# A chunked decay attention with an eight-expert mixture: w1 gathered in two parts, the filling products taken out, the experts' order fitted anew

## The chip, the cores and the metric

One core of a Trainium2 chip runs the program. The metric is the device time of one launch in microseconds (us). Five engines work side by side, each through a queue of its own in a fixed order: TensorE (PE, matrix products; PEld are its weight loads), VectorE (DVE), ScalarE (ACT), GpSimd (POOL) and SyncE (SP, which only issues transfers here). Semaphores hold an instruction until what it needs is done.

## The reference

Two parts. The first is a linear attention with a complex decay, for B=4, H=8, S=768 positions and D=48; its output, as `x`, has N=3072 tokens of 384 numbers. The second sends each token to one of eight experts, each of which takes exactly `cap` = 384 tokens.

```python
for t in range(S):
    S_re, S_im = ar*S_re - ai*S_im + kv, ar*S_im + ai*S_re
    y[:, :, t] = einsum('bhd,bhde->bhe', q[:, :, t], S_re)
x = y.transpose(0, 2, 1, 3).reshape(3072, 384)
for idx in argsort(-(x @ w_gate).flatten()):       # best score first
    tok, e = idx // 8, idx % 8
    if assigned[tok] < 0 and counts[e] < 384:
        assigned[tok] = e; counts[e] += 1
for e in range(8):
    out[assigned == e] = relu(x[assigned == e] @ w1[e]) @ w2[e]
```

`w1[e]` is 384 x 1024 and `w2[e]` 1024 x 384, in 32-bit floats.

## The kernel before, in words

**Attention (0 to some 228 us).** 24 pieces of 128 tokens. The recurrence over positions becomes products of blocks on TensorE. `store` (line 608) writes each piece's `x` to the array `xd` in DRAM, 128 rows of 384 numbers, from GpSimd for the first 21 pieces; the logits stay on the chip.

**Ranking.** The greedy rule is solved one expert after another, in the order in which the experts fill up, so which expert comes first is known only on the chip. `Router.find` (line 830) searches the score from which an expert takes all tokens, in rounds of 32 thresholds. In a round VectorE compares every token's key with the thresholds (`ind`), TensorE counts per expert and threshold (`cnt`), VectorE makes flags and their sum (`f`, `fm`), and TensorE adds the step to the thresholds of the next round (`thr`). For the first expert `ind` is made in three pieces, so that counting starts sooner. After the rounds follow the expert's number (`eidx`, as a row number for each of 128 partitions), ties, and each token's place (`pi`). `Router.slots` (line 1030) turns places into lists of 384 token numbers, `idx`: VectorE builds one-hot factors (`hl`, `o`, `rh`), TensorE multiplies them (`cnt`), VectorE adds four partial sums where the product came in four groups (`ic`, four steps) and casts to integers (`idx`).

**Gathers.** `route` (line 1350) issues an expert's transfers on GpSimd, all indirect: `w1t`, one row of 3 x 1024 numbers for each of 128 partitions (1.57 MB), by `eidx`; three times 128 token rows from `xd`, by a column of `idx` each (`xg`); and `w2t`, 1.57 MB by `eidx`, for experts 0 to 2 after the rows.

**First expert.** `first_expert` (line 1419) works in plain 32-bit floats, 128 tokens at a time: `turn` transposes the rows on TensorE against `ident`, ScalarE copies them (`x`); `hidden` multiplies with `w1t`, eight blocks of 128 hidden features with three products each; `last` multiplies with `w2t`, and GpSimd scatters the rows to `out`. A plain 32-bit product runs as two passes, so its record counts twice (x6 for three products).

**Experts 1 to 7.** 384 tokens at once. Each operand is split in a high and a low part (`split`: ScalarE makes the high one, VectorE subtracts), and a product is three products of these parts: `xh,w1h`, `xl,w1h`, `xh,w1l`, then `w2h,hl` and so on. `w1` is split in three pieces of 1024 columns, one for each third of the 384 input features, so all three pieces must be there before a block of hidden features is complete.

**Filling and warm-up products.** `fill` (line 788) puts products of one constant into a spare accumulator, behind which the next useful product is made to wait. `FILLS` (line 1508) gives the numbers: 24 before the first round; in each round 5 after the counts and 7 after the new thresholds, 14 after the last ones; and 36 while VectorE makes places. `WARM` = 14 (line 1507) products of `mask` with `ident` stand between the first slot products and the first turn, the loop being at line 1466. Nobody reads the result of either.

**What sets the order.** In the expert half every operation is recorded (all at line 140) with its estimated duration. `rank` gives each a due time by the way that remains behind it, less an offset by its kind from the table `M_OFF` (line 1503; kinds are `find3`, `slot2`, `w1s`, `tp` and so on). `in_order` then plays the engines through and issues on each the ready operation with the smallest number. So the table decides which of two ready steps comes first, on every engine. The attention has a table of its own, which the change leaves alone.

Of the kernel before, what the change touches and what calls it, by code (L numbers as in the profile page):

```python
# [8 lines left out]
F32 = mybir.dt.float32  # L9
# [13 lines left out]
N, DM, E, FF = B * S, H * D, 8, 1024  # L23
CAP = N // E
NT = N // 128
GC = 3
T = GC * 128
FK = FF // 128
# [218 lines left out]
def attention(nc, real, tc, z, kq_in, a_re, a_im, v_in, xd, later):  # L247
# [261 lines left out]
    def unit(i):  # L509
# [204 lines left out]
class Router:  # L714
# [72 lines left out]

    def fill(self, n, after):

        with self.nc.one():  # L790
            for _ in range(n):
                self.nc.tensor.matmul(self.hot, self.z.tri, self.z.tri, start=True, stop=True)
        o = self.nc.ops[-1]
        o.kind = "fill"
        if after is not None:
            o.deps.append(after)
        self.filled = [o]

    def scale(self):
# [30 lines left out]
    def find(self, parts, by_pe, more):  # L830
# [5 lines left out]
        def t(n, shape, dt=F32, **k):  # L836
            return wk.tile(shape, dt, name=n, **k)
# [7 lines left out]
        if first:  # L845
            begin()
            self.fill(FILLS[0], nc.ops[-1])
        thr = self.thr
        lots = list(zip(parts, parts[1:] + (NT,)))
        for it in range(len(GRID)):  # L850
# [3 lines left out]
            for n, (lot, stop) in enumerate(lots):  # L854
                some = ind[:, lot:stop]
                some.part = n
                v.tensor_tensor(some, bc(m[:, lot:stop], 32),
                                thr[:, None, 32 * it:32 * it + 32].to_broadcast([128, stop - lot, 32]), op=OP.is_ge)
                with nc.one() as group:
# [22 lines left out]
            for lo, hi in ((at, at + 32), (at + 32, end + 1)) if first and at < end else ((at, end + 1),):  # L882
                nc.tensor.matmul(thr[:, lo:hi], self.weight[:, it].to_broadcast([128, 128]), fm_.bitcast(BF)[:, 1:2].to_broadcast([128, hi - lo]),
                                 start=False, stop=(it == len(GRID) - 1), skip_group_check=True)
                if first:
                    nc.ops[-1].deps += self.filled
            if first:
                self.fill(FILLS[2 if at < end else 3], nc.ops[-1])

# [19 lines left out]
        v.tensor_scalar(s1, self.pidm, lop[:32], lo[:32], op0=OP.add, op1=OP.is_equal)  # L909
        with nc.one() as group:  # L910
            if not by_pe:
                closing()
            counts()
        if first:
            group[0].deps += self.filled
            nc.kind = "lead"
# [29 lines left out]
        nc.tensor.matmul(off, z.tri, rt.rearrange("p a b -> p (a b)").bitcast(BF)[:, 1::2], start=True, stop=True)  # L946
        if first:
# [82 lines left out]
    def slots(self, pi, by_pe):  # L1030
# [19 lines left out]
        for h in range(2):  # L1050
# [9 lines left out]
            self.placed = group[0]  # L1060
            if self.filled:
                group[0].deps += self.filled
        self.filled = []
        idx = t("idx", [128, 3], I32, bufs=8)
# [216 lines left out]
def experts(nc, tc, z, router, w1, w2, xd, out):  # L1281
# [50 lines left out]
    hot = pm.tile([128, 3, 128], F32, name="acc", bufs=5)  # L1332
    router.hot = hot[:, 0]
    idx, w1s, w2t, latest = {}, {}, {}, []

    w1t0 = wp.tile([128, 3, FF], F32, name="w1t", bufs=2)
    xg0 = wk.tile([128, 3, DM], F32, name="xg")
# [12 lines left out]
    def route(e):  # L1350
# [8 lines left out]
        eidx, pi = router.found  # L1359
        w1t = w1t0 if e == 0 else wp.tile([128, 3, FF], F32, name="w1t", bufs=2)  # L1360
# [52 lines left out]
    def settle():  # L1413
# [3 lines left out]
        settled.append(o)  # L1417

    def first_expert(xg):

# [10 lines left out]
        def hidden(j):  # L1431
            for f0 in range(0, FK, 3):
                n = min(3, FK - f0)
                hp = pm.tile([128, 3, 128], F32, name="acc", bufs=5)
                for i in range(n):
                    col = slice((f0 + i) * 128, (f0 + i) * 128 + 128)
                    with plan.one():
                        whole(hp[:, i], [(w1s[0][:, kk, col], x0[:, j][:, kk]) for kk in range(3)])
                act(h0[:, j][:, f0:f0 + n], hp[:, :n], AF.Relu).kind = "h"
# [34 lines left out]
    for e in range(1, E):  # L1474
# [4 lines left out]
        for f in range(FK):  # L1479
            hp = pm.tile([128, CAP], F32, name="acc", bufs=5)  # L1480
            col = slice(f * 128, f * 128 + 128)
            product(hp, [([w[:, kk, col] for w in w1s[e]], [x[:, kk] for x in xs]) for kk in range(3)], True)
            hi, lo = (h[:, f] for h in hs)
# [18 lines left out]
M_LATE = 0.0  # L1502
M_OFF = {'close1': 4907.3801, 'close2': 3736.7957, 'close3': 12989.3501, 'close4': 4978.9595, 'close5': 20150.8396, 'close6': 7935.2835, 'find1': 910.3797, 'find2': -491.2383, 'find3': 12453.3585, 'find4': 936.189, 'find5': 1287.5239, 'find6': -3522.5781, 'find7': 2244.6658, 'fill': -40000.0, 'first': 30000.0, 'lead': 31000.0, 'h': -9561.514, 'mm': -23392.8927, 'next0': 2441.5673, 'next1': 11732.2633, 'next2': -9507.9749, 'next3': 3444.9243, 'next4': -9522.1411, 'next5': -1772.7047, 'next6': 766.1226, 'ot': 6939.8479, 'out': 3884.4579, 'place1': 5375.3134, 'place2': -4569.1293, 'place3': 4573.9198, 'place4': 7290.1175, 'place5': 798.3189, 'place6': 454.7009, 'slot1': 5720.6654, 'slot2': 3387.2087, 'slot3': -8030.2154, 'slot4': 6878.5738, 'slot5': -5200.2856, 'slot6': -10123.2603, 'slot7': -5245.0693, 'tp': -28295.1209, 'w1d': 3587.4164, 'w1s': -39661.3634, 'w2d': 14744.4273, 'w2s': -204656.3808, 'warm': -8694.1139, 'x': -5392.4881, 'xd': 5339.4823}
W1_POOL = ()
M_SLACK = 0.4
W2_POOL = {}
WARM = 14
FILLS = (24, 5, 7, 14, 36)
PARTS = ((0, 8, 16),) + 6 * ((0,),)
# [5 lines left out]
@with_exitstack  # L1515
def tile_decay_attention_then_capacity_moe(ctx, tc, kq, a_re, a_im, v, w_gate, w1, w2, out):
    nc = tc.nc
# [8 lines left out]
    attention(queue, nc, tc, z, kq, a_re, a_im, v, xd, router.constants())  # L1526
    experts(queue, tc, z, router, w1, w2, xd, out)


def _lay_out(inputs):  # L1530
# [7 lines left out]
    def in_pieces(a):  # L1538
# [4 lines left out]
    c = np.ascontiguousarray  # L1543
    v = inputs["v"].transpose(0, 1, 3, 2).reshape(B, 4, 2 * D, S // T, T).transpose(0, 3, 2, 1, 4)
    return {
        "kq": c(np.stack([feature_major(inputs["k"]), feature_major(inputs["q"])], axis=2)).reshape(G, 128, 6 * T),
# [3 lines left out]
        "w_gate": c(inputs["moe_w_gate"]).reshape(4, 2, D, E),  # L1550
        "w1": c(inputs["moe_w1"].reshape(E, 3, 128, FF).transpose(0, 2, 1, 3)).reshape(E * 128, 3 * FF),
        "w2": c(inputs["moe_w2"].reshape(E, FK, 128, DM).transpose(0, 2, 1, 3)).reshape(E * 128, FK * DM),
# [16 lines left out]
```

## Time and profile before

| | |
|---|---|
| three runs | 504.97, 505.26, 506.15 us (median 505.26) |
| profiled execution, its own time | 505.34 us |
| its span, from first to last instruction | 503.6 us |
| TensorE busy | 464.3 us (92%), 5284 instructions |
| TensorE weight loads | 406.2 us (81%) |
| VectorE busy | 406.6 us (81%) |
| ScalarE busy | 285.1 us (57%) |
| GpSimd busy | 84.3 us (17%) |

The shares are averages over stages with different limits, and products that nobody reads count as busy. "Granted clock" is the share of TensorE's full speed that the chip allows in a stretch: 1.00 stands for 2.4 GHz, 0.50 for 1.2 GHz. A row of a timeline reads: start, duration, engine, line, operation, result and operands with their shape, how many instructions are taken together, and in brackets how long the engine was idle before and what released it.

### The profile page before, as it was taken

To read this page: it belongs to the slowest core of one execution; us is meant where nothing else is said; L and a number is where in the kernel's file an instruction comes from. 1 tells how busy PE (TensorE), PEld (TensorE's weight loads), DVE (VectorE), ACT (ScalarE), POOL (GpSimd) and SP (SyncE) were. 2 spreads that over 40 slices of the span, in tenths; PEclk is the share of its full clock that TensorE was granted. 3 is DMA by queue.
4 is the path that set the end of the run, shared out by engine and by line. 5 is a ranking of instruction groups with operands and counts; after the bars stand their busy time and mean duration, and the time that the engine had idled before them with its cause. 6 is when DMAs were issued, how large, how long until landed. Compare 5 with 4: busy or idle time off the path is not lost.

```text
span 503.6 us, 12840 instructions
## 1 busy us (share of the span) xinstructions
PE 464.3 (92%) x5284; PEld 406.2 (81%) x5284; DVE 406.6 (81%) x1172; ACT 285.1 (57%) x470; POOL 84.3 (17%) x120
## 2 busy tenths in 40 slices
PE   0488999999999999998889999999999999999995
PEld 0276888888787988887888689888988889989995
DVE  7989999999999999636846799799898998937250
ACT  7999988999998974710021443154423444345341
POOL 2000000000010000000210411424121252350202
PEclk9999999999999999998799999999999999999999
DMA  7647877868578664520340723562070621780001
GB/s 269 202 143 192 302 243 215 267 208 291 170 214 283 223 189 126 162 81 19 140 159 1 268 79 134 191 240 94 33 297 33 267 79 45 278 316 21 31 17 48
DMA packets 26538, 82.70 MB, mean 164 GB/s; under 512 B 4096, under 2 KB 11136, under 8 KB 23408
## 3 DMA queue, kind: packets, MB, share of 16 engines
q1 hardware_dynamic: 19264, 42.55, 27.6%
q0 software_dynamic: 6784, 38.75, 21.4%
q8 instruction: 41, 0.67, 0.6%
q10 hardware_dynamic: 432, 0.59, 0.3%
q14 instruction: 17, 0.14, 0.1%
HBM read 53.49 MB, written 9.44 MB: 125 GB/s over the span
## 4 chain that ended last, share of the span: by engine, by line
PE 49%; DVE 18%; issue 13%; ACT 10%; DMA 4%; POOL 2%; SPq 1%; POOLq 1%; another core or an unknown queue 0%; DVEq 0%; ACTq 0%
PE acc L140 21%; PE y L140 7%; PE U L140 6%; PE sc L140 6%; ACT s L140 3%; PE vx L140 3%; PE sq L140 3%; DVE hl L140 2%; DVE f L140 2%; PE kp L140 2%; PE cnt L140 2%; ACT L271 2%; DMA w2t<-in_w,eidx 2%; DMA ai<-in_a_im 2%; POOL out L140 2%
## 5 line engine op out<-in xcount | busy, mean ns | idle before, releaser
L140 ACT ACTIVATE hh<-acc 128x384 fp32r<-128x384 f32 x56 | 27.5, 491 | 72.3 <-PE acc L140 71.8
L140 PE MATMUL acc<-w2h,hl 128*128 128x384 f32 x168 | 54.4, 346 | 0.0
L140 PE MATMUL acc<-w2l,hh 128*128 128x384 f32 x168 | 53.8, 346 | 0.5 <-DVE w2l L140 0.3
L140 PE MATMUL acc<-w2h,hh 128*128 128x384 f32 x168 | 53.9, 345 | 0.0
L140 PE MATMUL acc<-xh,w1h 128*128 128x384 f32 x168 | 52.3, 347 | 1.0 <-ACT w1h L140 0.7
L140 PE MATMUL acc<-xh,w1l 128*128 128x384 f32 x168 | 51.8, 346 | 0.0
L140 PE MATMUL sc<-KQ 96*128 96x128 f32 x384 | 50.4, 281 | 1.2 <-DVE am L140 1.2
L140 PE MATMUL acc<-xl,w1h 128*128 128x384 f32 x168 | 51.3, 343 | 0.0
L140 PEld LDWEIGHTS sc<-KQ 96*128 96x128 f32 x384 | 45.7, 191 | 5.0 <-DVE am L140 1.6
L140 POOL DMA_DIRECT2D xd<-x x21 | 11.4, 545 | 193.0 <-ACT LP L140 161.8
L140 PE MATMUL y<-vt,am 128*64 128x56 f32 x768 | 43.6, 224 | 0.0
L140 DVE SCALAR_TENSOR_TENSOR hl<-acc,hh 128x384 fp32r<-128x384 f32 x56 | 30.7, 551 | 15.7 <-ACT hh L140 14.3
L140 POOL DMA_INDIRECT out<-ot,idx x24 | 26.9, 1122 | 97.8 <-ACT ot L140 95.6
L140 DVE TENSOR_TENSOR f<-kq,CS 128x768 f32<-128x768 f32 x48 | 42.5, 949 | 0.5 <-ACT CS L140 0.3
L140 DVE TENSOR_TENSOR ind<-m,thr 128x768 bf16<-128x768 f32 (+1 forms) x45 | 34.0, 773 | 10.1 <-PE thr L140 7.7
L140 PEld LDWEIGHTS y<-vt,am 128*64 128x64 f32 x768 | 36.8, 137 | 3.9 <-issue 2.3
L140 PE MATMUL y<-W,KQ 96*64 96x56 f32 x640 | 38.5, 222 | 0.5 <-DVE W L140 0.5
L140 PE MATMUL sq<-s,ident 128*128 128x384 f32 x42 | 20.1, 563 | 17.3 <-ACT sq L140 17.3
L140 DVE TENSOR_TENSOR am<-sc,mask 128x512 f32<-128x512 f32 x48 | 31.9, 682 | 4.6 <-PE sc L140 4.2
L140 POOL DMA_INDIRECT xg<-xd,idx x24 | 25.9, 1078 | 51.6 <-DVE idx L140 24.8
L140 PEld LDWEIGHTS acc<-xh,w1h 128*128 128x128 f32 x168 | 31.1, 188 | 2.7 <-ACT w1h L140 1.0
L140 PEld LDWEIGHTS y<-W,KQ 96*64 96x64 f32 x640 | 32.6, 137 | 0.6 <-DVE W L140 0.6
(201 smaller groups left out, 1135.2 us busy)
## 6 DMA issues: line engine op xcount, KB each, us to landing
KQ<-f SPq DMA_DIRECT2D x64, 192.8 KB, 4.1
kq<-in_kq SPq DMA_DIRECT2D x8, 1152.0 KB, 8.6
KQ<-f SPq DMA_DIRECT2D x64, 96.4 KB, 3.1
V<-in_v SPq DMA_DIRECT2D x8, 576.0 KB, 4.9
xd<-x POOLq DMA_DIRECT2D x21, 192.0 KB
ar<-in_a_re SPq DMA_DIRECT2D x6, 576.0 KB, 4.4
ai<-in_a_im SPq DMA_DIRECT2D x6, 576.0 KB, 5.4
ar<-in_a_re SPq DMA_DIRECT2D x2, 384.0 KB, 3.2
```

The costliest lines, as they stand in the source:

```text
L140: r = f(*a, **k)
L271: real.scalar.add_instruction(ins)
```

## The change

- **w1 in two arrays.** The host lays `w1` out by pairs of hidden blocks: four chunks of 768 numbers for each partition, each with all three thirds of the input features for two hidden blocks. The first three chunks are the array `w1a`, the last is `w1b`. `route` gathers each by an indirect transfer of its own (1.18 and 0.39 MB). `weight(w, f, kk)` picks a block's factor.
- **The first expert's second part** is issued behind the first 128 token rows, and the other rows behind it; the order w1a, rows, w1b, rows, rows, w2 is forced by dependences. The later experts issue w1b right behind w1a.
- **Splits of w1** in four pieces of 768 columns, in place of three of 1024.
- **No filling products**: `fill`, `FILLS` and the waits behind them are gone.
- **Warm-up products** 10 in place of 14.
- **Two VectorE steps** (`e2`, `rs`) are written ahead of `of` in the ranking.
- **The first two stores** of `x` go in halves of 64 rows.
- **M_OFF** has other numbers throughout, and no `fill`.

```diff
         def store():
-            (nc.gpsimd if i < NT - 3 else nc.scalar).dma_start(xd[i * 128:i * 128 + 128], mine["x"].rearrange("p a b -> p (a b)"))
+            for a in (0, 64) if i < 2 else (0,):
+                b = a + 64 if i < 2 else 128
+                (nc.gpsimd if i < NT - 3 else nc.scalar).dma_start(
+                    xd[i * 128 + a:i * 128 + b], mine["x"][a:b].rearrange("p a b -> p (a b)"))
...
         if first:
             begin()
-            self.fill(FILLS[0], nc.ops[-1])
...
-                if first:
-                    group[0].deps += self.filled
-            if first:
-                self.fill(FILLS[1], nc.ops[-1])
...
-            if first:
-                self.fill(FILLS[2 if at < end else 3], nc.ops[-1])
...
         nc.tensor.matmul(off, z.tri, rt.rearrange("p a b -> p (a b)").bitcast(BF)[:, 1::2], start=True, stop=True)
-        if first:
-            self.fill(FILLS[4], nc.ops[-1])
-        of = t("of", [128, 2])
-        v.tensor_copy(of, off)
...
         v.scalar_tensor_tensor(rs, cc, -1.0, e2, op0=OP.mult, op1=OP.mult, accum_out=r)
+        of = t("of", [128, 2])
+        v.tensor_copy(of, off)
...
-        rows(w1t.rearrange("p a f -> p (a f)"), w1, eidx, 128 * 3 * FF * 4, "w1d")
+        def part(lo, hi):
+            def issue():
+                nc.gpsimd.indirect_dma_start(out=flat.real()[:, 768 * lo:768 * hi], out_offset=None, in_=w1[lo // 3],
+                                             in_offset=bass.IndirectOffsetOnAxis(ap=eidx.real(), axis=0))
+            move(issue, [w1t[:, c] for c in range(lo, hi)], [eidx], 128 * 768 * (hi - lo) * 4, "w1d")
+            return plan.ops[-2]
+        part(0, 3)
         if late:
             plan.ops[-2].deps.append(late)
+        if e:
+            part(3, 4)
...
             rows(xg[:, j], xd, i[:, j:j + 1], 128 * DM * 4, "xd")
+            if e == 0 and j == 0:
+                before = plan.ops[-2]
+                before = [before, part(3, 4)]
+                before[1].deps.append(before[0])
+            elif e == 0:
+                plan.ops[-2].deps.append(before[1])
...
-            w1s[e] = pair([128, 3, FF], "w1", 2)
-            for kk in range(3):
-                split(w1t[:, kk], *(w[:, kk] for w in w1s[e]), "w1s", g if (e, kk) in W1_POOL else v)
+            w1s[e] = pair([128, 4, 768], "w1", 2)
+            for c in range(4):
+                split(w1t[:, c], *(w[:, c] for w in w1s[e]), "w1s", g if (e, c) in W1_POOL else v)
...
+    def weight(w, f, kk):
+        at = (f % 2 * 3 + kk) * 128
+        return w[:, f // 2, at:at + 128]
...
-M_OFF = {..., 'fill': -40000.0, 'first': 30000.0, 'lead': 31000.0, 'h': -9561.514, 'mm': -23392.8927, ...}
+M_OFF = {..., 'first': -763.0821, 'h': -11761.0629, 'lead': 6417.3714, 'mm': -11170.5708, ...}
...
-WARM = 14
-FILLS = (24, 5, 7, 14, 36)
+WARM = 10
```

Three places show how the order moves. The first is TensorE's queue from the last counts of the second expert's first round to the first expert's first products. `mask` against `ident` are warm-up products, `ident,xg` the three transposes of the first 128 rows, `thr` the second expert's new thresholds. Ahead of these rows both kernels have eight more warm-up records. Before:

```order
L140 MATMUL cnt<-oh,ind 128x32
L140 MATMUL acc<-ident,mask 128x128 x6
L140 MATMUL acc<-ident,xg 128x128
L140 LDWEIGHTS weight
L140 MATMUL thr<-fm_163,weight 128x129
L140 MATMUL acc<-ident,xg 128x128 x2
L140 MATMUL acc<-x_3791,w1t 128x128 x3
```

With the change:

```order
L140 MATMUL cnt<-oh,ind 128x32
L140 MATMUL acc<-ident,mask 128x128 x2
L140 MATMUL acc<-ident,xg 128x128 x3
L140 LDWEIGHTS weight
L140 MATMUL thr<-fm_163,weight 128x129
L140 MATMUL acc<-x_3657,w1t 128x128 x6
L140 LDWEIGHTS ind
```

Four warm-up products fewer stand before the transposes, and the three transposes now stand together ahead of `thr`.

The second is GpSimd's queue at the first expert's gathers. Before, with the second expert's `w1t` behind them:

```order
L140 DMA w1t<-in_w,eidx 128x3072
L140 DMA xg<-xd,idx 128x384 x3
L140 DMA w2t<-in_w,eidx 128x3072
L140 DMA w1t<-in_w,eidx 128x3072
L140 DMA out<-ot,idx 3072x384
```

With the change:

```order
L140 DMA w1t<-in_w1a,eidx 128x2304
L140 DMA xg<-xd,idx 128x384
L140 DMA w1t<-in_w1b,eidx 128x768
L140 DMA xg<-xd,idx 128x384 x2
L140 DMA w2t<-in_w,eidx 128x3072
L140 DMA w1t<-in_w1a,eidx 128x2304
L140 DMA w1t<-in_w1b,eidx 128x768
L140 DMA out<-ot,idx 3072x384
```

Two issues more stand ahead of the first scatter, one of them between the first rows and the others.

The third is VectorE's queue where the third expert's (expert 2's) slot sums `ic` become `idx`. `hl` is the low part of expert 1's hidden features, `w2l` that of its second weights, `cs` and `f` belong to the ranking of the expert after. Before:

```order
L140 TENSOR_TENSOR ic<-cnt,ic 32x12
L140 SCALAR_TENSOR_TENSOR hl<-acc,hh 128x384
L140 TENSOR_TENSOR cs_167<-cnt,need 32x8
L140 SCALAR_TENSOR_TENSOR hl<-acc,hh 128x384
L140 TENSOR_TENSOR cs_167<-cnt,cs_167 32x8
L140 SCALAR_TENSOR_TENSOR hl<-acc,hh 128x384
L140 TENSOR_TENSOR cs_167<-cnt,cs_167 32x8
L140 TENSOR_TENSOR w2l<-w2t,w2h 128x384
L140 TENSOR_TENSOR cs_167<-cnt,cs_167 32x8
L140 TENSOR_TENSOR w2l<-w2t,w2h 128x384
L140 TENSOR_SCALAR f_159,fm_163<-cs_167 32x8
L140 CAST idx<-ic 32x3 x4
```

With the change:

```order
L140 TENSOR_SCALAR ic<-cnt 32x12
L140 TENSOR_TENSOR oh<-oh,free 128x192
L140 TENSOR_TENSOR ic<-cnt,ic 32x12
L140 SCALAR_TENSOR_TENSOR hl<-acc,hh 128x384
L140 TENSOR_TENSOR ic<-cnt,ic 32x12
L140 SCALAR_TENSOR_TENSOR hl<-acc,hh 128x384
L140 TENSOR_TENSOR ic<-cnt,ic 32x12
L140 SCALAR_TENSOR_TENSOR hl<-acc,hh 128x384
L140 CAST idx<-ic 32x3 x4
```

The cast moved up ahead of the ranking's four `cs` and its `f` and of two `w2l`; one `hl` is left between the last sum and the cast.

## Rows read from the trace of the kernel before

**Rows 1.** Busy time by stretch: us, busy (instructions) per engine, clock, DMA, GB/s.

```profile
230.50:235.70 5.20, 4.99 (x96) 4.20 (x97) 4.15 (x22) 0.00 (x0) 0.22 (x2) 1.00 0.08 27
235.70:246.00 10.30, 10.28 (x148) 9.42 (x146) 7.44 (x51) 0.00 (x0) 1.02 (x1) 0.50 0.05 14
246.00:255.50 9.50, 6.23 (x87) 5.67 (x86) 6.54 (x27) 0.49 (x1) 3.82 (x4) 1.00 0.73 246
255.50:296.00 40.50, 40.12 (x294) 31.64 (x295) 28.57 (x124) 13.43 (x28) 7.51 (x8) 1.00 0.38 135
296.00:498.00 202.00, 197.76 (x1269) 182.29 (x1268) 155.62 (x574) 79.93 (x162) 55.55 (x51) 1.00 0.37 132
```

**Rows 2.** Timeline of VectorE, first ranking: start us, us, instruction, idle before and releaser.

```profile
233.82 1.08 DVE L140 TENSOR_TENSOR ind<-m,thr 128x256 bf16<-128x256 int32 x3 [0.24 <-PE thr L140]
...
235.44 0.07 DVE L140 DVE_READ_ACCUMULATOR f<-cnt 32x1 f32 x1
...
235.82 1.08 DVE L140 TENSOR_TENSOR ind<-m,thr 128x256 bf16<-128x256 int32 x3 [0.23 <-PE thr L140]
...
237.46 0.07 DVE L140 DVE_READ_ACCUMULATOR f<-cnt 32x1 f32 x1
...
238.07 1.08 DVE L140 TENSOR_TENSOR ind<-m,thr 128x256 bf16<-128x256 int32 x3 [0.46 <-PE thr L140]
...
246.64 0.30 DVE L140 TENSOR_TENSOR rh<-o,token 128x288 f16<-128x288 f16 x1
```

**Rows 3.** Timeline of TensorE, first ranking to second turn, same columns.

```profile
235.57 0.21 PE L140 MATMUL thr<-fm,weight 128*128 128x32 bf16 x2
...
237.77 0.26 PE L140 MATMUL thr<-fm,weight 128*128 128x32 bf16 x2
...
247.35 0.76 PE L140 MATMUL cnt<-rh,o 128*32 128x12 f16 x24
...
248.04 2.05 PE L140 MATMUL acc<-ident,mask 128*128 128x128 f32 x16
...
251.67 0.32 PE L140 MATMUL cnt<-oh,ind 128*128 128x32 bf16 x6 [1.57 <-DVE ind L140]
...
253.42 0.39 PE L140 MATMUL acc<-ident,xg 128*128 128x128 f32 x2
...
255.50 0.94 PE L140 MATMUL acc<-x,w1t 128*128 128x128 f32 x6 [1.69 <-ACT x L140]
...
261.68 0.74 PE L140 MATMUL acc<-ident,xg 128*128 128x128 f32 x5
```

**Rows 4.** Timeline of GpSimd, gathers of the first expert.

```profile
243.93 1.02 POOL L140 DMA_INDIRECT w1t<-in_w,eidx  x1 [12.25 <-DVE tie L140]
249.07 0.98 POOL L140 DMA_INDIRECT xg<-xd,idx  x1 [4.12 <-DVE idx L140]
250.35 0.95 POOL L140 DMA_INDIRECT xg<-xd,idx  x1 [0.30 <-issue]
```

**Rows 5.** Busy time by stretch, columns as in rows 1: weight gather.

```profile
248.50:249.50 1.00, 1.00 (x12) 1.00 (x11) 0.92 (x4) 0.00 (x0) 0.43 (x1) 1.00 0.94 393
```

**Rows 6.** Timeline of ScalarE, copies of turned rows.

```profile
254.96 0.49 ACT L140 ACTIVATE x<-acc 128x384 f32<-128x384 f32 x1 [25.54 <-PE acc L140]
...
262.13 0.87 ACT L140 ACTIVATE x<-acc 128x384 f32<-128x384 f32 x2
```

**Rows 7.** Waits of TensorE from 296 to 498: us in total, times, longest.

```profile
PE acc L140 <- DMA xg<-xd,idx: 0.9, 1, 0.9
PE acc L140 <- ACT w1h L140: 0.7, 1, 0.7
```

**Rows 8.** Timeline of TensorE in expert 1, which turns expert 2's rows.

```profile
319.28 0.44 PE L140 MATMUL acc<-ident,xg 128*128 128x128 f32 x2 [0.93 <-DMA xg<-xd,idx]
```

**Rows 9.** Timeline of VectorE before expert 2's row gathers.

```profile
311.01 0.54 DVE L140 TENSOR_TENSOR w2l<-w2t,w2h 128x384 fp32r<-128x384 f32 x1
...
311.55 0.67 DVE L140 CAST idx<-ic 32x3 int32<-32x3 f32 x4
```

More of the change, by code (lines that the diff above doesn't have):

```diff
@@ L786, in mine @@
         return self.nc.wrap(self.con.tile(shape, dt, name=n), dt)
[L788 to L797, printed above, removed]
     def scale(self):
@@ L858, in find @@
                                 thr[:, None, 32 * it:32 * it + 32].to_broadcast([128, stop - lot, 32]), op=OP.is_ge)
-                with nc.one() as group:
+                with nc.one():
                     for c in range(0, stop - lot) if by_pe else ():
@@ L884, in find @@
                                  start=False, stop=(it == len(GRID) - 1), skip_group_check=True)
-                if first:
-                    nc.ops[-1].deps += self.filled
-            if first:
-                self.fill(FILLS[2 if at < end else 3], nc.ops[-1])
         def closing():
@@ L909, in find @@
         v.tensor_scalar(s1, self.pidm, lop[:32], lo[:32], op0=OP.add, op1=OP.is_equal)
-        with nc.one() as group:
+        with nc.one():
             if not by_pe:
@@ L914, in find @@
         if first:
-            group[0].deps += self.filled
             nc.kind = "lead"
@@ L946, in find @@
         nc.tensor.matmul(off, z.tri, rt.rearrange("p a b -> p (a b)").bitcast(BF)[:, 1::2], start=True, stop=True)
-        if first:
-            self.fill(FILLS[4], nc.ops[-1])
-        of = t("of", [128, 2])
-        v.tensor_copy(of, off)
         r = t("r", [128, 1])
@@ L1060, in slots @@
             self.placed = group[0]
-            if self.filled:
-                group[0].deps += self.filled
-        self.filled = []
         idx = t("idx", [128, 3], I32, bufs=8)
@@ L1332, in experts @@
     hot = pm.tile([128, 3, 128], F32, name="acc", bufs=5)
-    router.hot = hot[:, 0]
     idx, w1s, w2t, latest = {}, {}, {}, []
-    w1t0 = wp.tile([128, 3, FF], F32, name="w1t", bufs=2)
+    w1t0 = wp.tile([128, 4, 768], F32, name="w1t", bufs=2)
     xg0 = wk.tile([128, 3, DM], F32, name="xg")
@@ L1359, in route @@
         eidx, pi = router.found
-        w1t = w1t0 if e == 0 else wp.tile([128, 3, FF], F32, name="w1t", bufs=2)
+        w1t = w1t0 if e == 0 else wp.tile([128, 4, 768], F32, name="w1t", bufs=2)
         late = e == E - 1 and latest[-1]
-        rows(w1t.rearrange("p a f -> p (a f)"), w1, eidx, 128 * 3 * FF * 4, "w1d")
+        flat = w1t.rearrange("p a f -> p (a f)")
+        def part(lo, hi):
[5 more added lines that the diff above has]
+        part(0, 3)
         if late:
             plan.ops[-2].deps.append(late)
+        if e:
+            part(3, 4)
         def second():
@@ L1435, in hidden @@
                 for i in range(n):
-                    col = slice((f0 + i) * 128, (f0 + i) * 128 + 128)
                     with plan.one():
-                        whole(hp[:, i], [(w1s[0][:, kk, col], x0[:, j][:, kk]) for kk in range(3)])
+                        whole(hp[:, i], [(weight(w1s[0], f0 + i, kk), x0[:, j][:, kk]) for kk in range(3)])
                 act(h0[:, j][:, f0:f0 + n], hp[:, :n], AF.Relu).kind = "h"
@@ L1480, in experts @@
             hp = pm.tile([128, CAP], F32, name="acc", bufs=5)
-            col = slice(f * 128, f * 128 + 128)
-            product(hp, [([w[:, kk, col] for w in w1s[e]], [x[:, kk] for x in xs]) for kk in range(3)], True)
+            product(hp, [([weight(w, f, kk) for w in w1s[e]], [x[:, kk] for x in xs]) for kk in range(3)], True)
             hi, lo = (h[:, f] for h in hs)
@@ L1502 @@
 M_LATE = 0.0
-M_OFF = {'close1': 4907.3801, 'close2': 3736.7957, 'close3': 12989.3501, 'close4': 4978.9595, 'close5': 20150.8396, 'close6': 7935.2835, 'find1': 910.3797, 'find2': -491.2383, 'find3': 12453.3585, 'find4': 936.189, 'find5': 1287.5239, 'find6': -3522.5781, 'find7': 2244.6658, 'fill': -40000.0, 'first': 30000.0, 'lead': 31000.0, 'h': -9561.514, 'mm': -23392.8927, 'next0': 2441.5673, 'next1': 11732.2633, 'next2': -9507.9749, 'next3': 3444.9243, 'next4': -9522.1411, 'next5': -1772.7047, 'next6': 766.1226, 'ot': 6939.8479, 'out': 3884.4579, 'place1': 5375.3134, 'place2': -4569.1293, 'place3': 4573.9198, 'place4': 7290.1175, 'place5': 798.3189, 'place6': 454.7009, 'slot1': 5720.6654, 'slot2': 3387.2087, 'slot3': -8030.2154, 'slot4': 6878.5738, 'slot5': -5200.2856, 'slot6': -10123.2603, 'slot7': -5245.0693, 'tp': -28295.1209, 'w1d': 3587.4164, 'w1s': -39661.3634, 'w2d': 14744.4273, 'w2s': -204656.3808, 'warm': -8694.1139, 'x': -5392.4881, 'xd': 5339.4823}
+M_OFF = {'close1': 21139.6573, 'close2': 7314.2043, 'close3': 12942.22, 'close4': 11690.8262, 'close5': 6863.2998, 'close6': -451.5483, 'find1': -3704.0335, 'find2': -1916.3891, 'find3': -67.7544, 'find4': 4806.073, 'find5': -1681.1192, 'find6': -3654.3032, 'find7': -11609.9588, 'first': -763.0821, 'h': -11761.0629, 'lead': 6417.3714, 'mm': -11170.5708, 'next0': -5975.6657, 'next1': -4106.9594, 'next2': -158.233, 'next3': -10211.75, 'next4': -5088.7055, 'next5': -17234.0147, 'next6': -1009.421, 'ot': 401.8857, 'out': 333.4749, 'place1': 6801.0462, 'place2': 6417.4987, 'place3': 8870.8733, 'place4': 6634.6636, 'place5': -9432.3868, 'place6': 7743.1919, 'settle': 7563.6529, 'slot1': 12159.7359, 'slot2': 1416.9124, 'slot3': 5587.3936, 'slot4': -2743.7043, 'slot5': 3927.6614, 'slot6': 8368.2895, 'slot7': 7183.0966, 'tp': -37525.3228, 'w1d': 7842.4279, 'w1s': -24592.7515, 'w2d': 1176.6931, 'w2s': -21874.9893, 'warm': -5299.0651, 'x': -2358.03, 'xd': 1891.4784}
 W1_POOL = ()
@@ L1515, in tile_decay_attention_then_capacity_moe @@
 @with_exitstack
-def tile_decay_attention_then_capacity_moe(ctx, tc, kq, a_re, a_im, v, w_gate, w1, w2, out):
+def tile_decay_attention_then_capacity_moe(ctx, tc, kq, a_re, a_im, v, w_gate, w1a, w1b, w2, out):
     nc = tc.nc
@@ L1526, in tile_decay_attention_then_capacity_moe @@
     attention(queue, nc, tc, z, kq, a_re, a_im, v, xd, router.constants())
-    experts(queue, tc, z, router, w1, w2, xd, out)
+    experts(queue, tc, z, router, (w1a, w1b), w2, xd, out)
 def _lay_out(inputs):
@@ L1544, in _lay_out @@
     v = inputs["v"].transpose(0, 1, 3, 2).reshape(B, 4, 2 * D, S // T, T).transpose(0, 3, 2, 1, 4)
+    w1 = inputs["moe_w1"].reshape(E, 3, 128, FK, 128).transpose(0, 2, 3, 1, 4).reshape(E * 128, 3 * FF)
     return {
@@ L1550, in _lay_out @@
         "w_gate": c(inputs["moe_w_gate"]).reshape(4, 2, D, E),
-        "w1": c(inputs["moe_w1"].reshape(E, 3, 128, FF).transpose(0, 2, 1, 3)).reshape(E * 128, 3 * FF),
+        "w1a": c(w1[:, :2304]),
+        "w1b": c(w1[:, 2304:]),
         "w2": c(inputs["moe_w2"].reshape(E, FK, 128, DM).transpose(0, 2, 1, 3)).reshape(E * 128, FK * DM),
```

## The prediction

> **What bounds the kernel now.** I read the busy time by stretch first, to see which stretch has which limit. From 296 us to the end of the products TensorE is busy for 197.76 of 202.00 us [rows 1]: the seven later experts are a queue on TensorE, and only a wait inside that queue can be won there. The first expert (255.5 to 296) is the same, 40.12 of 40.50. Between 230.5 and 255.5, where tokens are ranked and the first expert's rows fetched, the same column tells nothing, because up to 246 most of TensorE's work is filling products, which nobody reads. There I read VectorE's timeline. One round of the ranking is: three `ind` pieces, their counts on TensorE, `f`, and `thr`, which starts the next round. Rounds start at 233.82, 235.82 and 238.07 [rows 2]: 2.00 us, then 2.25. The granted clock explains the step only in part: it is 1.00 (2.4 GHz) up to 235.7, 0.50 (1.2 GHz) from there to 246, and 1.00 again [rows 1]. It fell while the short fills (5 and 7) ran between the counts, and rose after the long ones (14 and 36).
>
> After the ranking three steps follow in a row: the slot products `cnt` give `idx`; GpSimd issues the row gathers from `idx`; TensorE turns the first 128 rows, ScalarE copies them (`x`), and the first expert's products begin at 255.50 [rows 3]. That start is what the first half of the change can move. From there on TensorE is a queue, so what starts earlier should end earlier.
>
> **The change, part by part.** The sum is made against the profiled execution's own 505.34 us; the median of the runs shown is 505.26, so 0.08 lies between them.
>
> *Stores in halves.* The first two stores become four, on GpSimd, which does little else in the first half; nobody waits for them there: 0.
>
> *Fills in the rounds.* In the quick round `fm` is read out from 235.44 to 235.51 and `thr` starts at 235.57, 0.06 later; in the slow one it is ready at 237.53 and `thr` starts at 237.77, 0.24 later, because five fills at the lower clock stand ahead of it [rows 2, 3]. Without fills each of the three rounds at the lower clock gets 0.18 back: 0.54. The clock will fall earlier, since TensorE now does less; the two quick rounds then pay what the slow one pays besides the fills, 2.25 - 2.00 - 0.18 = 0.07 each, 0.14. Net gain 0.40.
>
> *Fills before the slot products.* `rh` is ready at 246.94 but the 24 products start at 247.35, behind 36 fills [rows 2, 3]. Free of them they start at about 247.0 and end some 0.3 earlier (their second half waits for one more VectorE step). One short VectorE step (`open`, about 0.1) now stands ahead of this chain: net 0.2. The row gathers come 0.40 + 0.2 = 0.6 earlier: the issue at 249.07 moves to 248.5 [rows 4].
>
> *The weight gather.* Now it is issued at 243.93, and the stretch from 248.5 to 249.5 moves 393 GB/s [rows 4, 5]. Its index moves up too, ahead of four VectorE steps. A quarter of 1.57 MB less is 0.39 MB, or 1.0 us; with the 0.6 above the first part is in about 1.6 us before the whole is now, and the first rows no longer queue behind it: they land before TensorE asks. The second part (chunk 4 of 4, for the last two of eight hidden blocks) is issued 1.3 us after the first rows and needed some 4 us into the products: hidden. The rows for the second and third turn, and `w2t`, go out 1.3 later against 0.6 earlier; the second turn comes 6 us after the first products [rows 3], so this is hidden too, and costs up to 0.7 if that cover goes.
>
> *Warm-up products.* 28 half-products (16 + 12) become 20 (16 + 4). 16 ran in 2.05 us at the upper clock, with their start [rows 3]. Now the clock is at its lower level when they begin, near 247.6, so 16 take up to 3.6 us and end at 251.2. That is about when the next ranking's `cnt` may start (251.67 less 0.6). Then that group, four half-products and the three transposes, all at the lower clock, 0.3 + 0.9 + 0.6: the transposes end at 253.0, where they end at 253.81 now [rows 3]. Gain 0.8.
>
> *The pause before `x`.* The transposes' rows end at 253.81, yet ScalarE is released only at 254.96, 1.15 us later. The second turn's transposes, 261.68 to 262.42, let the copies start at 262.13 [rows 3, 6]. I can't say what holds the first ones back. They stand at the moment when gathered rows land, so the pause may come again: between 0 and 1.15. I take 0.2, by the nearest row, the second turn: gain 0.95 more.
>
> *Clock in the first products.* They start at 253.75 instead of 255.50. The last fills ran from about 242.4 until the clock rose at 246.0 [rows 1]; the warm-up from 247.6 on is as dense, so the rise should come near 251 to 254. Bounds: no loss, or the first 48 half-products (255.50 to 261.5, 6.0 us) all at half speed, 6.0 lost. I take 0.3, for a rise soon after 254.
>
> Here the Trainium skill speaks against the change. "TensorE: Matmul & The Clock Gate", section "Why this matters for your kernels", asks to keep TensorE free of idle gaps or have its clock drop. The rows say that the fills did not prevent that: the clock was at 0.50 from 235.7 to 246 with them running. By that rule alone the first products would lose; by the rows, the warm-up brings the clock back.
>
> *Later experts.* TensorE is idle for 4.2 us of 202 there [rows 1]; the wait list names gathered rows with 0.9 and `w1h` with 0.7 [rows 7]. The first is plainly touched: 0.93 us in expert 2, at 319.28 [rows 8]. VectorE cast that `idx` only at 311.55 [rows 9]: in the old order ten steps of other work stand between the last slot sum and the cast, in the new one a single `hl`. Between the first sum and the cast there were fourteen such steps and are four; the two `w2l` among the ten that go are 0.54 us each, so `idx` comes more than 1 us earlier, and that wait goes: 0.9. The wait for `w1h` should shrink, as a hidden block now needs one chunk of four instead of three of three. The refitted order moves everything else; I price it by the rest of the idle time, gone or doubled: between -3.3 and +3.3 beside the 0.9, taken as 0. The second weight gather adds one GpSimd issue of 1.3 us per expert ahead of the rows' issue; where rows are late that is its price, inside this bound. Four chunk splits hold as many columns as three do now; VectorE has 46 us idle of 202 [rows 1] to hide one more start each.
>
> The skill's page "DMA: Bandwidth & Descriptors", section "Rules for kernel authors", also speaks against splitting a transfer: the page gives its fixed cost as about 2.0 us, so eight more gathers would be 16 us by an estimate from it, if each stood on the path. The trace has neighbouring gathers issued 1.3 us apart while earlier bytes still move [rows 4], so they overlap.
>
> Sum: 505.34 - 0.8 - 0.95 + 0.3 - 0.9 = **503.0 us**.
>
> **Rivals.**
> (B) *The pause returns and the refit gives nothing.* Only the 0.8 stays, less 0.3 for the clock: 504.8, no change. For it: the pause has no cause in the trace. Against: the second turn goes without it.
> (C) *Slower by the clock.* Without fills TensorE enters the first products at its lower level and stays there, because turn, copy and waits break its run. The gain of 1.75 is eaten once the rise comes 3.5 us into the products; in their middle it gives 505.34 - 1.75 + 3.0 = 506.6, at their end 509.6. For it: the clock was down for 10 us though fills ran. Against: between 246 and 255.5 TensorE was busy for only 6.23 of 9.50 us and the clock stayed up [rows 1].
> (D) *The new order or the extra gathers make later experts wait.* Rows late by 1.3 us in two or three experts, or the idle time doubled: 505.34 - 1.45 + 3.3 = 507.2.
> (E) *Everything goes well:* the clock is back before the turn and half of the other idle time goes: 503.0 - 0.3 - 1.6 = 501.1 or less.
>
> **How the numbers follow.** My forecast gets 0.44 (501.4 to 504.4), B 0.23 (504 to 505.6), C 0.11, D 0.11, E 0.11. The range 500.9 to 505.9 leaves out the far parts of C, D and E, about 0.2. A measurement of this kernel can tell 0.2%, 1.0 us. Faster by more: E 0.11, nine tenths of the forecast 0.40, half of B 0.11, a little of D 0.02: 0.64. Slower: most of C and over half of D, 0.16. The rest, 0.20, is no change.
>
> **What would show it.** Rounds 2.05 to 2.1 us apart, all at the lower clock; slot products right behind `rh`; first products starting at 253 to 254.5; the clock at 1.00 before 255; no wait for `xg` in expert 2. It is wrong if the first products start later than 255, if they run at 0.50 for more than 3 us, or if TensorE's idle time after 296 grows beyond its 4.2 us of now [rows 1].

## The result and the profile after

The changed kernel took 500.59 us in the median of four runs (499.08 to 501.64), the kernel before 505.52 us beside it: ratio 0.9902, interval 0.9884 to 0.992. It is faster by 4.9 us, about twice the 2.3 us that were forecast, and lies 0.3 us below the range. The profiled execution is the fastest of the four (499.08 us against 505.34 us before), so the pair of profiles differs by 6.3 us, more than the medians do; where the slower runs lose the rest no trace shows.

The page of the changed kernel:

```profile
span 497.3 us, 12595 instructions
...
PE 454.8 (91%) x5149; PEld 398.2 (80%) x5149; DVE 408.0 (82%) x1179; ACT 285.6 (57%) x477; POOL 94.1 (19%) x130
```

Its busy time by stretch, columns as in rows 1:

```profile
230.50:235.70 5.20, 2.59 (x51) 2.04 (x52) 4.16 (x23) 0.00 (x0) 0.22 (x2) 0.79 0.11 37
235.70:246.00 10.30, 4.91 (x84) 3.91 (x83) 7.92 (x53) 0.00 (x0) 1.03 (x1) 0.50 0.08 18
246.00:250.60 4.60, 3.63 (x37) 3.71 (x38) 4.39 (x17) 0.00 (x0) 1.58 (x2) 0.50 0.59 233
250.60:253.60 3.00, 1.97 (x19) 1.36 (x17) 1.42 (x8) 0.49 (x1) 2.23 (x3) 1.00 0.63 202
...
253.60:492.84 239.24, 236.48 (x1562) 213.78 (x1562) 185.98 (x704) 93.73 (x195) 71.82 (x66) 1.00 0.38 137
```

TensorE now idles half of the time up to 246.0, the clock is at its lower level until 250.6, and it is back 3 us ahead of the first products. The same stretch before, from the first expert's first product to the end of the last product:

```profile
255.50:498.02 242.52, 237.90 (x1562) 213.93 (x1562) 184.18 (x697) 93.36 (x188) 63.06 (x58) 1.00 0.37 133
```

The same 1562 records take 3.28 us less: 1.86 less idle time (4.62 to 2.76) and 1.42 less busy time. The records of the experts' split products last some 345 ns and start some 190 ns apart, and their ends are modelled, so a start that comes up to 150 ns late is counted as busy time; that the 1.42 us are such short delays is likely, but not shown. TensorE's timeline answers to [rows 3]:

```profile
246.97 0.79 PE L140 MATMUL cnt<-rh,o 128*32 128x12 f16 x24 [2.21 <-DVE rh L140]
247.69 3.42 PE L140 MATMUL acc<-ident,mask 128*128 128x128 f32 x16
251.32 0.32 PE L140 MATMUL cnt<-oh,ind 128*128 128x32 bf16 x6 [0.21 <-DVE oh L140]
251.48 0.69 PE L140 MATMUL acc<-ident,mask 128*128 128x128 f32 x4
252.04 0.52 PE L140 MATMUL acc<-ident,xg 128*128 128x128 f32 x3
...
253.60 1.60 PE L140 MATMUL acc<-x,w1t 128*128 128x128 f32 x12 [0.72 <-issue]
...
492.50 0.34 PE L140 MATMUL acc<-w2h,hl 128*128 128x384 f32 x1
```

The first products start at 253.60, where they started at 255.50, though the ranking began 0.11 later (230.61 against 230.50). The last one ends at 492.84, and the span 4.46 us after it; before these were 498.02 and 5.54. So the 6.3 us are 1.9 at the start, 3.3 in TensorE's queue (the records from the first expert's first product to the last one) and 1.1 behind the last product. Waits of TensorE from 290 us on, which answer to [rows 7]:

```profile
PE acc L140 <- DVE hl L140: 0.7, 1, 0.7
PE cnt L140 <- DVE rh L140: 0.4, 1, 0.4
```

The whole list before was this, with the two rows of [rows 7] in place of the dots:

```profile
PE cnt L140 <- DVE rh L140: 0.9, 2, 0.6
...
PE thr L140 <- DVE f L140: 0.5, 1, 0.5
PE acc L140 <- DVE hl L140: 0.4, 2, 0.2
PE acc L140 <- DVE w2l L140: 0.3, 1, 0.3
```

### The profile page after: what moved, and what is told of

Read it like the earlier page. It is cut to its first block, busy times and chain, and to the rows that moved or that the text cites. A ratio compares the mean times of both kernels' runs of the same rounds, so it can differ in the third digit from the quotient of the medians.

```text
span 497.3 us, 12595 instructions
## 1 busy us (share of the span) xinstructions
PE 454.8 (91%) x5149; PEld 398.2 (80%) x5149; DVE 408.0 (82%) x1179; ACT 285.6 (57%) x477; POOL 94.1 (19%) x130
## 4 chain that ended last, share of the span: by engine, by line
PE 56%; DVE 22%; ACT 10%; issue 8%; DMA 2%; POOL 1%; POOLq 0%; SPq 0%; DVEq 0%
PE acc L140 25%; PE y L140 7%; PE U L140 7%; PE sc L140 6%; PE vx L140 3%; ACT s L140 3%; DVE hl L140 3%; PE sq L140 3%; DVE f L140 2%; PE cnt L140 2%; PE kp L140 2%; ACT L271 2%; DVE w2l L140 2%; DVE ind L140 2%; ACT CS L140 1%
## 5 line engine op out<-in xcount | busy, mean ns | idle before, releaser
L140 PE MATMUL acc<-xh,w1h 128*128 128x384 f32 x168 | 55.5, 345 | 1.0 <-DVE hl L140 0.7
L140 PE MATMUL acc<-xl,w1h 128*128 128x384 f32 x168 | 54.7, 343 | 0.0
L140 PE MATMUL acc<-xh,w1l 128*128 128x384 f32 x168 | 54.5, 342 | 0.0
L140 PE MATMUL acc<-w2h,hl 128*128 128x384 f32 x168 | 53.3, 344 | 0.0
L140 POOL DMA_DIRECT2D xd<-x x23 | 12.4, 542 | 192.1 <-ACT LP L140 160.9
L140 ACT ACTIVATE ot<-acc 128x384 f32<-128x384 f32 x24 | 11.8, 490 | 61.4 <-PE acc L140 57.5
```

Of the source, the lines that this page charges most:

```text
L140: r = f(*a, **k)
```

## The experiments

Ten edited kernels, and the changed kernel twice more, ran in three groups of four, the first on chip 10, the others on chip 8. The kernel before took 503.05 to 503.36 us beside them, against 505.52 in the first comparison, whose chip is not on record, so ratios to it are compared. Each was profiled once. Three lengths from TensorE's timeline say where a profile differs: the *start*, from the ranking's first product (`thr` from `start`) to the first expert's first product; the *queue*, from there to the end of the last product; the *tail*, from there to the end of the span.

| kernel | start | queue | tail | median | ratio (interval) |
|---|---|---|---|---|---|
| before, first profile | 25.0 | 242.5 | 5.5 | | |
| changed, first profile | 23.0 | 239.2 | 4.5 | 500.59 | 0.9902 (0.9884 to 0.992) |
| whole_stores | 22.6 | 237.8 | 5.2 | 498.82 | 0.9911 (0.9895 to 0.9927) |
| old_table | 22.0 | 242.5 | 4.5 | 500.90 | 0.9958 (0.9944 to 0.9973) |
| fills_back | 25.6 | 237.9 | 4.5 | 500.41 | 0.9940 (0.9924 to 0.9955) |
| late_fills | 22.6 | 237.8 | 4.5 | 497.51 | 0.9895 (0.9878 to 0.9912) |
| after_again | 23.2 | 237.8 | 4.5 | 497.41 | 0.9888 (0.9871 to 0.9904) |
| no_fills | 22.9 | 241.2 | 5.6 | 501.88 | 0.9980 (0.9969 to 0.9991) |
| w1b_first | 23.2 | 237.8 | 4.5 | 497.69 | 0.9899 (0.9883 to 0.9915) |
| lead_late | 22.1 | 237.8 | 4.5 | 497.11 | 0.9884 (0.9867 to 0.9902) |
| halves_only | 23.9 | 241.1 | 4.8 | 502.28 | 0.9982 (0.9970 to 0.9994) |
| no_fills_new_table | 23.0 | 252.3 | 5.6 | 510.61 | 1.0161 (1.0127 to 1.0195) |
| lead_warm8 | 22.0 | 237.8 | 4.5 | 497.31 | 0.9896 (0.9872 to 0.992) |
| after_third | 23.0 | 237.7 | 4.5 | 497.53 | 0.9896 (0.9875 to 0.9918) |

**The changed kernel again (after_again, after_third).** No edit.

> The changed kernel itself once more, beside the other kernels of this group. From the ranking's first product (thr from start) to the first expert's first product 22.5 to 23 us (25.0 before the change), from there to the last product 239.2 us (242.5 before), tail 4.5 us; ratio to the kernel before 0.988 to 0.992. If the stretch of 239.2 us were chance of one execution, it would come out at 241 or more here.

> The changed kernel a third time, to stand beside the others of this group: ratio 0.988 to 0.991, start 22.9 to 23.2 us, stretch 237.7 to 239.3, tail 4.5.

Start and tail came as in the first profile. The queue is 1.4 us shorter than there, and that of the old order too (241.1 and 241.2 in halves_only and no_fills against 242.5). Laid side by side, record by record, the old order's 1.3 to 1.4 us lie mostly at one place, the wait for `w1h` in expert 6, which halves_only and no_fills lack; the new order's lie at three places, 0.4 to 0.5 at each. So the sums agree and the places do not, and why the first profiles lose time there is open. Between the two orders lie 3.3 to 3.5 us either way. On chip 8 the first expert takes 33.1 to 33.2 us in both orders, and all of the gain is behind it: 208.0 us in no_fills, 204.7 in after_again.

**The tail: stores whole again, and stores in halves alone.** whole_stores on the changed kernel, halves_only the reverse on the kernel before:

```diff
-            for a in (0, 64) if i < 2 else (0,):
-                b = a + 64 if i < 2 else 128
+            for a in (0,):
+                b = 128
```

> Only the first two stores go whole again, as before the change. Theory: the two extra stores shift which completion semaphore the last scatter signals, and SyncE waits for these one after another at the end, so the tail from the last product to the end of the span goes from 4.5 us (changed kernel) back to 5.3 to 5.6 us; time 0.8 to 1.1 us above the changed kernel. Rival (the shorter tail is chance, or comes from the other program length): tail stays at 4.4 to 4.7 us and the time does not move by more than 0.3 us.

> The kernel before with nothing changed but the first two stores in halves. Theory: the last scatter then signals the completion semaphore that SyncE waits for last, as in the changed kernel; tail 4.5 to 4.8 us instead of 5.55, time 0.8 to 1.1 us below the kernel before (ratio about 0.998), start and queue untouched. Rival (the halves do nothing by themselves): tail 5.5 us, no gain.

The tails are 5.24 and 4.84 us, both by 0.1 or less outside what was expected, and the halves alone make the kernel before some 0.9 us faster (ratio 0.9982, by its interval 0.3 to 1.5). The time of whole_stores (0.9911) points the same way, but its interval overlaps with those of the changed kernel. The raw records of SyncE's last waits show why. Columns: start, end, the semaphore waited for; some later records are left out. Each transfer issued on GpSimd signals one of eight semaphores in turn (107 to 114 in the records). Before, where the last scatter signals 113:

```
454.61 501.45 113
501.49 501.52 112
501.55 501.58 111
501.62 501.65 110
501.71 501.74 109
501.79 501.82 108
502.18 502.21 107
502.26 502.29 100
502.32 502.35 104
```

With the change, where it signals 107:

```
493.09 493.12 109
493.17 493.20 108
493.56 496.28 107
496.33 496.36 100
496.39 496.42 104
```

SyncE waits for 113 first and for 107 seventh (not last, as the expectation for halves_only has it), one after another. The last scatter is seen 3.4 us after the last product in both (501.45 - 498.02, 496.28 - 492.84). Before, eight waits still had to be gone through, 0.90 us; now two, 0.14. Eight more gathers turn the eight semaphores once round and change nothing; the two more stores move the last scatter on by two, from 113 over 114 to 107. In whole_stores it signals 113 again and the eight waits take 0.90 us. Behind the last of these waits 1.2 us follow in the kernel before and in halves_only, 0.9 in the changed kernel and in whole_stores: so the other 0.3 us goes with the rest of the change, and its cause is open.

**The queue: table and layout.** old_table is the changed kernel with the old numbers; no_fills_new_table is the kernel before with `FILLS` all 0, `WARM` 10 and the new numbers.

```diff
-M_OFF = {..., 'first': -763.0821, 'h': -11761.0629, 'lead': 6417.3714, ...}
+M_OFF = {..., 'first': 30000.0, 'h': -9561.514, 'lead': 31000.0, ...}
```

> The changed kernel with the old table of offsets. Theory: the refitted order gave the 3.3 us between the first product and the last one; with the old table that stretch goes from 239.2 us back to 242 or more, and the time is 3 us or more above the changed kernel (about 504). Rival (w1 in four chunks gave it, so that the blocks wait less for their splits): stretch 239 to 240 us, time within 1 us of the changed kernel. First products start at 253 to 254.5 by either.

> The kernel before without fills, with 10 warm-up products, w1 whole in one gather and three splits, but the new table of offsets. Theory A (the table is worth something only together with the layout and the instruction list it was fitted to): stretch from first to last product 241 us or more. Rival B (the new offsets are better by themselves): 238 to 239 us. Tail 5.5 us by both, as the stores are whole.

The old table on the new layout takes 242.5 us for the queue, 1.3 more than on the old layout on such chips (241.2); the new table on the old layout 252.3, 11 more. Only the pair that was fitted together gives 237.8. So the new layout is worth nothing in the queue with the old numbers, and the new numbers are worth nothing with the old layout; which part of the layout the new numbers need was not tried. By the ratios old_table is 3.1 to 3.5 us slower than the changed kernel (0.9958 against 0.9896 and 0.9888), though its start is shorter (22.0 us). Waits of TensorE in no_fills_new_table from 250 us on, the longest four rows:

```profile
PE acc L140 <- ACT xh L140: 2.5, 1, 2.5
PE acc L140 <- DVE w2l L140: 2.1, 2, 1.9
PE cnt L140 <- DVE rh L140: 2.0, 2, 1.4
PE acc L140 <- DVE hl L140: 1.7, 4, 0.6
```

Three of these stand in the list of the kernel before, only shorter; the longest, for `xh`, does not. TensorE is idle for 11.3 of the 252.3 us here, against 4.0 of 241.2 in no_fills. Part of the 11 us is clock: it fell to 0.50 twice within this queue.

```profile
374.70:378.12 3.42, 2.98 (x9) 2.74 (x9) 2.66 (x9) 0.00 (x0) 3.12 (x2) 0.50 0.20 58
408.84:412.25 3.41, 3.41 (x13) 3.10 (x12) 2.31 (x8) 0.00 (x0) 1.95 (x2) 0.50 0.45 123
```

By an estimate from these rows, half of the 6.8 us, 3.4 us, is the most that this can cost.

**The start: fills.** no_fills is the kernel before with `FILLS` all 0 and `WARM` 10; fills_back puts all fills and 14 warm-up products into the changed kernel.

```diff
-FILLS = (24, 5, 7, 14, 36)
+FILLS = (0, 0, 0, 0, 0)
-WARM = 14
+WARM = 10
```

> The kernel before, only without filling products and with 10 warm-up products. Theory: rounds 0.2 us shorter and free slot products bring the first products to 23.3 to 24 us after the ranking's first product (25.0 with fills), the stretch to the last product stays at 242.5 and the tail at 5.5, as neither the order nor the stores change; time 1 to 1.7 us below the kernel before. Rival (the clock, down from 233 to 250 without fills, takes it back in the warm-up and first products): no gain, within 0.4 us.

> The changed kernel with all filling products and 14 warm-up products as before; the order of everything else is nearly the same. Theory: rounds 2.2 us instead of 2.05 and slot products behind the last fills, so the first products start 1.5 to 2 us later than in the changed kernel (about 255), but the clock is back at 1.00 by 247 in every run; so all runs lie within 0.6 us of each other, and the median, 500.5 to 501.2, is about that of the changed kernel. Rival (the fills cost 1.9 us and buy nothing): median 502 to 502.8.

Without fills the start is 22.9 us, the same as in the changed kernel, though no_fills gathers `w1` whole. With them it depends on the clock: in the old order it is 25.0 in the first profile and 23.9 in halves_only, in the new one 25.6 in fills_back. The clock in fills_back and then in halves_only, both with the same fills:

```profile
236.00:249.60 13.60, 13.32 (x184) 12.11 (x182) 9.58 (x59) 0.00 (x0) 1.03 (x1) 0.50 0.24 89
```

```profile
236.00:244.00 8.00, 7.11 (x137) 5.74 (x135) 5.75 (x38) 0.00 (x0) 0.28 (x1) 1.00 0.01 2
244.00:247.60 3.60, 3.60 (x36) 3.60 (x37) 3.60 (x26) 0.00 (x0) 0.74 (x1) 0.53 0.60 188
```

Fills hold back the useful products behind them: `rh` is ready at 247.51 in fills_back, but its products start at 249.13, behind the last fills. Where the clock stays up longer they cost less: the one run of fills_back with a mean clock of 0.995 took 498.85 us, the four with 0.986 took 500.40 to 500.73. Taking the fills out, together with four warm-up products, gains 1.0 to 2.1 us of start in the old order by the profiles, and 1.0 us by the ratio of no_fills (0.9980, by its interval 0.5 to 1.6). In the new order fills_back loses 2.5 us against after_again in the profiles' starts and queues, and 2.6 by the ratios (0.9940 against 0.9888). So the expectation's theory failed: the clock was not back by 247, the runs lie 1.9 us apart, and the fills buy nothing, as the rival says. Its median of 500.41 is below the rival's 502, but the kernel before is 2.5 us faster on this chip as well (503.05 against 505.52).

**The order of the first gathers.** w1b_first is the changed kernel with the first expert's second part issued right behind the first:

```diff
         part(0, 3)
-        if e:
-            part(3, 4)
+        part(3, 4)
```

(the dependences that put it behind the first rows go too).

> The changed kernel, but the first expert's second weight part goes out right behind the first part, ahead of the first rows, so that all 1.57 MB stand ahead of them again. Theory A: the first rows land about 1 us later and the first products start 0.5 to 1 us later than in the changed kernel. Rival B: at the lower clock the warm-up products end only at 251 to 252, about when the rows land anyway, so the start moves by less than 0.2 us and the time does not move.

B holds: 497.69 against 497.41 us in the same group, the intervals overlap, and the start is 23.2 us in both. GpSimd in w1b_first, and what TensorE did there at that time:

```profile
243.17 1.02 POOL L140 DMA_INDIRECT w1t<-in_w1a,eidx  x1 [11.61 <-DVE ah L140]
244.50 0.98 POOL L140 DMA_INDIRECT w1t<-in_w1b,eidx  x1 [0.30 <-issue]
248.48 0.95 POOL L140 DMA_INDIRECT xg<-xd,idx  x1 [3.01 <-DVE idx L140]
```

```profile
247.46 3.79 PE L140 MATMUL acc<-ident,mask 128*128 128x128 f32 x16
251.09 0.34 PE L140 MATMUL cnt<-oh,ind 128*128 128x32 bf16 x6
251.27 1.20 PE L140 MATMUL acc<-ident,mask 128*128 128x128 f32 x4
252.26 0.63 PE L140 MATMUL acc<-ident,xg 128*128 128x128 f32 x3
```

By the transfers' records all of w1 is in by 249.91 here, and the first rows 1.2 us later, at 251.13 (after_again: 251.37). TensorE turns them only at 252.26, because the warm-up products at the lower clock stand in front. The first gather is early enough; the order of the two parts decides nothing here.

**Trying for more (late_fills, lead_late, lead_warm8).** Fills only in TensorE's long idle times, 14 and 18; then 8 and 20 with the old offsets for the first ranking (`first` 30000, `lead` 31000); then without the last two warm-up products as well.

> The changed kernel with fills only where TensorE has nothing to do for long: 14 behind the last round's thresholds and 18 before the slot products. Theory: the clock comes back at 245 to 248 instead of 250.6 to 258, no useful product is held, the first products start at 253.0 to 253.5 at full clock in every run: median 498.5 to 499.3, all runs within 0.6 us. Rival (runs differ for another reason than the clock's rise): median 500 to 501 with the same spread of 2.5 us; or, if the fills hold up the slot products, first products at 254 and 499.8.

> The changed kernel with the old table's two offsets for the first expert's ranking steps (so that its VectorE steps come in the old order, from which slot products began 0.5 us sooner), and fills only in TensorE's long idle times (8 and 20). The order behind the first expert is untouched. Theory: first products 21.5 to 22.2 us after the ranking's first product, stretch 239.2, tail 4.5: about 1 us below the changed kernel, ratio 0.987 to 0.9885. Rival (the start is set by the landing of the first rows or by the warm-up products, not by the slot products): no better than the changed kernel.

> As lead_late, but the last two of the ten warm-up products are not issued (they keep their place in the plan, so nothing else moves). They stand between the second expert's counts and the first turn, 0.6 to 0.7 us, after the rows have landed at 251.1. Theory: first products 21.5 to 21.8 us after the ranking's first product, 0.3 to 0.6 below lead_late, ratio to the kernel before about 0.9875. Rival (the clock comes back later for want of them, or the turn waits for something else): no better than lead_late.

The late fills did not bring the clock back at 245 to 248: it rose at 250.2 in late_fills, at 250.6 in the changed kernel's first profile. The old offsets did make the start 0.9 to 1.0 us shorter in the profiles, but the medians are 0.3 us below after_again and 0.2 below after_third, within the intervals. Without the last two warm-up products TensorE waited 0.45 us for the first rows instead, so lead_warm8 is no better than lead_late, as its rival says. No kernel tried is measurably faster than the changed one.

## Why the prediction was right or wrong

*Start: right in the profile.* Forecast 1.75 us, 1.90 in the profile. With queue and tail as in the profiles, the medians' 4.9 us would leave only some 0.5 for it. Rounds start at 233.98, 236.03 and 238.05, 2.05 and 2.02 apart:

```profile
233.98 1.08 DVE L140 TENSOR_TENSOR ind<-m,thr 128x256 bf16<-128x256 int32 x3 [0.28 <-PE thr L140]
236.03 1.08 DVE L140 TENSOR_TENSOR ind<-m,thr 128x256 bf16<-128x256 int32 x3 [0.25 <-PE thr L140]
238.05 1.08 DVE L140 TENSOR_TENSOR ind<-m,thr 128x256 bf16<-128x256 int32 x3 [0.23 <-PE thr L140]
...
246.61 0.30 DVE L140 TENSOR_TENSOR rh<-o,token 128x288 f16<-128x288 f16 x1
```

The slot products follow `rh` (ready at 246.91) at 246.97; the first rows were issued at 248.71 (forecast 248.5), the 16 warm-up half-products took 3.42 us (forecast 3.6), and the first products began at 253.60 (forecast 253.75). That this came so close is in part luck: the transposes ended at 252.56, 0.4 ahead of the forecast, as the clock rose before them, and the pause before `x` shrank only to some 0.5 us, to ScalarE's start at 253.06, where 0.2 was taken. What made the pause of 1.15 us stays open.

*Clock: right in the profiles, perhaps not in all runs.* It was back at 250.6 in the first profile, 252.8 and 252.0 in the two others, ahead of the first products each time: 0 lost, 0.3 forecast. The first comparison's runs of 499.08, 499.98, 501.19 and 501.64 us have mean clocks of 0.982, 0.979, 0.974 and 0.975, so the longer times go with more time at the lower clock. By an estimate from these means the two slowest runs spent some 25 us at 0.50, the profiled one 18; if the 7 more followed 250.6, the clock rose behind the start of the first products and the 0.3 was too little there. No trace shows where they lie. Rival C in its full form was not seen. On the Trainium skill's advice against idle gaps ("TensorE: Matmul & The Clock Gate", "Why this matters for your kernels"): without fills the clock fell some 2 us sooner (233.5 against 235.7), but with them it fell too, behind 5.2 us in which TensorE was busy for 4.99 [rows 1], and in fills_back it stayed at 0.50 with TensorE busy for 13.32 of 13.60 us.

*Later experts: the step that failed.* "I price it by the rest of the idle time, gone or doubled: between -3.3 and +3.3 beside the 0.9, taken as 0." The whole term was 0.9; the runs show 3.3 to 3.5. The mechanism, a refitted order that moves short steps up, was right, and the term for it was too small. The 0.9 for `xg` in expert 2 came, and no wait for it is left in the list. But the waits for `f` and `w2l` went as well, that for `rh` fell from 0.9 to 0.4 (it is gone in after_again and after_third), and only that for `hl` grew, from 0.4 to 0.7. The wait for `w1h` is no part of it, as halves_only and no_fills, in the old order, do not have it either. The bound had held this, the value taken had not: four of the six rows of the old list were waits for VectorE, whose order the table sets, and none of these four had been looked up in the new order. The 1.42 us less of busy time (1.25 between no_fills and after_again) were in no view that was read.

*Stores in halves: wrong by 0.7 to 0.9 us.* "Nobody waits for them there: 0." Nobody does; but two more transfers shift which semaphore the last scatter signals, more than 430 us later. The end of the span behind the last product was never priced; in all 1.1 us went there.

*Weight gather: right, and less useful than told.* "Hidden" held for the second part: by the transfers' records it was in by 253.41, ahead of the first products. The first rows no longer stood behind it either: the first part was in by 248.71, the rows by 251.37. But in w1b_first, with all of `w1` ahead of them, they were in by 251.13, so putting the second part behind them was not needed.

*Range.* Start, queue and tail all came out on the good side: rival E, which had 501.1 or less at 0.11. In the profile the clock was back before the turn, as E has it; beside the 0.9 another 2.4 us left the queue, where E has 1.6; and the tail came besides.

## What to carry to other kernels

Where a table that sets the order is fitted anew, price every wait of the bottleneck engine, not the one that you recognise: look each up in both orders, and count it as gone where the step it waits for has moved up. Such a table belongs to its list of instructions; used with another list it made the kernel 1.6% slower than before. Read what stands between the last useful instruction and the end of the program, down to which semaphore the last transfer signals.

## What the runs showed of the hardware that was not expected

The number of transfers issued on GpSimd, counted round eight semaphores, sets part of the time at the program's end: the closing waits stood in the same order in all four kernels looked at, and the eight behind a last transfer on 113 took 0.90 us, the two behind one on 107 took 0.14. With the same fills in the ranking, the clock was at 0.50 for 13.65 us in fills_back, 10.2 in the kernel before and some 3.4 in halves_only, so keeping TensorE busy there did not fix its level. The same program's queue came out 1.4 us longer in one profile than in another, by one to three single waits.
